# Cached attention on one core: two quarters of wo between the last V blocks, and row sums in two wide products

## The chip, the cores and the metric

The kernel runs on one core of a Trainium2 chip. The metric is the time of one execution in device microseconds, the median over several runs; less is better. The profile is one execution recorded by the hardware profiler; its times are counted from the first instruction, and the span from the first to the last instruction is a little shorter than the time of the execution.

## The reference

Grouped attention over a cache, for 8 sequences of 4 new tokens each. 32 query heads share 8 K/V heads of width 128, with 2048 cached positions. All is bfloat16.

```python
B, Sq, D = 8, 4, 512
Hq, Hkv, Sk, Dh = 32, 8, 2048, 128

def reference(x, k_cache, v_cache, wq, wo):
    q = (x @ wq).reshape(B, Sq, Hq, Dh).transpose(0, 2, 1, 3)
    k = jnp.repeat(k_cache, Hq // Hkv, axis=1)
    v = jnp.repeat(v_cache, Hq // Hkv, axis=1)
    scores = jnp.einsum("bhqd,bhkd->bhqk", q, k) * (Dh ** -0.5)
    p = jax.nn.softmax(scores, axis=-1)
    o = jnp.einsum("bhqk,bhkd->bhqd", p, v)
    return o.transpose(0, 2, 1, 3).reshape(B, Sq, Hq * Dh) @ wo
```

K and V are 32 MB each, wq and wo 4 MB each; every byte of them is read once. The output is 32 KB.

## The kernel before

**Units and steps.** Two K/V heads of one sequence make a unit: 32 units, numbered u, ordered by head pair p (4 of them, `G2`) and then by sequence b (8). A unit's K is one tile of 128 partitions by 32 columns of 128 values (`k_sb`, 1 MB, one DMA, line 87), and its V the same (`v_sb`, line 97). A unit is worked in two halves of 16 columns. The main loop (line 264) runs over `step`, one half of a unit in each: 64 steps (`NH`) and a lead of 7. In one step TensorE transposes K of half `step + 7` (`transpose_part`, line 163, in two parts), computes the scores of half `step + 6` (line 179), and, with the exponentials ready by then, the values of half `step` (line 199). In the second half of a unit it first computes the row sums (`norms`, line 213), and after the values VectorE normalises (`finish`, line 230).

**The engines.** The order on each engine is the order of the text; the schedule is manual. The transposed K goes from PSUM to SBUF as `kt` by VectorE (line 168), and in one of four cases by ScalarE (line 166). ScalarE computes the exponentials into `probs` (line 185). The scores are written with the positions on the partitions, so the sum over positions is a product of `probs` with a matrix of ones: it gives every partition the same sums. `norms` takes the 32 columns of a unit in groups of `LC = 8`, each group one product of 256 columns accumulated into `l_ps`; VectorE then adds the 8 groups (line 221) and takes the reciprocal (line 225).

**The output projection.** When a head pair is done, `to_tokens` (line 242) transposes its eight heads to have tokens on the partitions and copies them to `nat_sb` (line 248), and `to_wo_rows` (line 257) transposes them back with the rows in the order in which wo is loaded, copied to `oP[p]` (line 262). For the first three pairs this is done in the main loop, in the steps of the next pair's second and third sequence. `project` (line 297) multiplies `oP[p]` with quarter p of wo, eight products of 512 columns, all accumulated into `out_ps`.

**The loads.** All go through SyncE's queue, in the order of a list: K of unit u together with V of unit u - 3, from one list that runs until all V are in. `load_ready` is called at the end of each step and lets out what has a free buffer: 7 for K, 6 for V. At most eight DMAs are under way. When the list is empty (step 51), the loads of wo follow: three of 1 MB, one of 512 KB and two of 256 KB (`load_wo`, line 104). After the loop stand the last pair's transposes, the 32 products of `project`, two casts (lines 313 and 314) and the store.

PSUM is used in four pools: `psum_k` for the transposed K (3 buffers), `psum_s` for scores and for `out_ps` (2), `psum_o` (2), and `psum_l` (1) for the row sums, `nat` and `perm` in turn.

Of the kernel before, what the change touches and what calls it, by code (L numbers as in the profile page):

```python
# [9 lines left out]
FP32 = mybir.dt.float32  # L10
# [4 lines left out]
def kernel(  # L15
# [9 lines left out]
    nc = tc.nc  # L25

    B, Sq, D = x.shape
    _, Hkv, Sk, Dh = k_cache.shape
# [3 lines left out]
    T = B * Sq  # L32
    R = D // 128
    G2 = Hkv // 2
    C = 2 * Sk // 128
    NQ = 2 * rep * Sq
# [3 lines left out]
    NU = G2 * B  # L40
    NH = 2 * NU
# [4 lines left out]
    WR = HP  # L46
    DH = D // 2
    AX = mybir.AxisListType.X
    LC = 8
    ADD = mybir.AluOpType.add  # L50
    assert Dh == 128 and C == 32 and NQ == 32

    const = ctx.enter_context(tc.tile_pool(name="const", bufs=1))
    kpool = ctx.enter_context(tc.tile_pool(name="kpool", bufs=KB))
# [4 lines left out]
    psum_s = ctx.enter_context(tc.tile_pool(name="psum_s", bufs=2, space=bass.MemoryType.PSUM))  # L59
# [11 lines left out]
    wo_sb = const.tile([128, G2, WR, D], BF16, name="wo_sb")  # L71
    out_sb = const.tile([T, D], BF16, name="out_sb")
    oP = [const.tile([128, WR, T], BF16, name=f"oP{p}") for p in range(G2)]
# [28 lines left out]
    def load_wo(p, r0, n):  # L102
        rows = wo[p * HP * 128 : (p + 1) * HP * 128, :].rearrange("(q r) j -> q r j", r=WR)
        nc.sync.dma_start(wo_sb[:, p, r0 : r0 + n, :], rows[:, r0 : r0 + n, :])
# [3 lines left out]
    loads = []  # L108
    for u in range(NU + KA):
        if u < NU:  # L110
            loads.append(("k", u))
        if u >= KA - 1 and u - KA + 1 < NU:
            loads.append(("v", u - KA + 1))
    loads.reverse()

    def load_ready(nk, nv):

        while loads:
            kind, u = loads[-1]
            if u >= (nk + KB if kind == "k" else nv + VB):  # L120
                return
            loads.pop()
            (load_k if kind == "k" else load_v)(u)

    load_ready(0, 0)

    make_identity(nc, ident[:])
# [10 lines left out]
    for p in range(G2):  # L138
        psq = psum_s.tile([128, HP, T], FP32, tag="s", name="psq")
        for h in range(HP):  # L140
            hh = p * HP + h
            for r in range(R):
                nc.tensor.matmul(  # L143
                    psq[:, h, :],
                    lhsT=wq_sb[:, r, hh * 128 : (hh + 1) * 128],
                    rhs=xT_sb[:, r, :],
                    start=(r == 0),
                    stop=(r == R - 1),
# [9 lines left out]
    def transpose_part(i, part):  # L158
        u, hf = divmod(i, 2)
        c0 = hf * HC + part * (HC // 2)  # L160
        kp = psum_k.tile([128, HC // 2, 128], BF16, tag="k", name="kp")
        for c in range(HC // 2):
            nc.tensor.transpose(kp[:, c, :], ks[u][:, c0 + c, :], ident[:, :])  # L163
        k_t = ktpool.tile([128, HC // 2, 128], BF16, tag="kt", name="kt")
        if part == 1 and hf == 1:
            nc.scalar.copy(out=k_t[:, :, :], in_=kp[:, :, :])  # L166
        else:
            nc.vector.tensor_copy(out=k_t[:, :, :], in_=kp[:, :, :])  # L168
        kt[(i, part)] = k_t

    def scores(i):
        u, hf = divmod(i, 2)
        p, b = units[u]
        pr = probs[u % len(probs)]
        s_ps = psum_s.tile([128, HC, NQ], FP32, tag="s", name="s_ps")
        q2 = qT_all[:, p, b, :, :].rearrange("d h s -> d (h s)")
        for c in range(HC):
            k_t = kt[(i, c // (HC // 2))]
            nc.tensor.matmul(  # L179
                s_ps[:, c, :], lhsT=k_t[:, c % (HC // 2), :], rhs=q2, start=True, stop=True  # L180
            )
        for g in range(2):
            rows = slice(g * 64, (g + 1) * 64)
            cols = slice(g * NQ // 2, (g + 1) * NQ // 2)
            nc.scalar.activation(  # L185
                out=pr[rows, hf * HC : (hf + 1) * HC, cols], in_=s_ps[rows, :, cols], func=EXP
            )
# [3 lines left out]
    def values(i):  # L191
        u, hf = divmod(i, 2)
        p, b = units[u]
        pr = probs[u % len(probs)]
        if hf == 0:
            o_ps[u] = psum_o.tile([128, NQ], FP32, tag="o", name="o_ps")
        for c in range(HC):
            cc = hf * HC + c
            nc.tensor.matmul(  # L199
                o_ps[u][:, :],  # L200
                lhsT=vs[u][:, cc, :],
                rhs=pr[:, cc, :],
                start=(cc == 0),
                stop=(cc == C - 1),
            )
# [3 lines left out]
    def norms(u):  # L209
        pr = probs[u % len(probs)]  # L210
        l_ps = psum_l.tile([128, LC, NQ], FP32, tag="l", name="l_ps")
        for c in range(0, C, LC):
            nc.tensor.matmul(  # L213
                l_ps[:, :, :],
                lhsT=ones[:, :],
                rhs=pr[:, c : c + LC, :],
                start=(c == 0),
                stop=(c + LC == C),
            )
        l_sb = small.tile([128, NQ], FP32, tag="l_sb", name="l_sb")  # L220
        nc.vector.tensor_reduce(  # L221
            out=l_sb[:, :], in_=l_ps[:, :, :].rearrange("d c q -> d q c"), axis=AX, op=ADD
        )
        r_sb = small.tile([128, NQ], FP32, tag="r_sb", name="r_sb")
        nc.vector.reciprocal(r_sb[:, :], l_sb[:, :])  # L225
        r_sbs[u] = r_sb

    def finish(u):
        p, b = units[u]
        nc.vector.tensor_tensor(  # L230
            out=oT_all[:, p * HP : (p + 1) * HP, b, :],
            in0=o_ps[u][:, :].rearrange("d (h s) -> d h s", h=HP),
            in1=r_sbs[u][:, :].rearrange("d (h s) -> d h s", h=HP),
            op=mybir.AluOpType.mult,
        )
# [3 lines left out]
    def to_tokens(p):  # L239
        nat = psum_l.tile([T, HP, 128], BF16, tag="l", name="nat")  # L240
        for h in range(HP):
            nc.tensor.transpose(  # L242
                nat[:, h, :],
                oT_all[:, p * HP + h, :, :].rearrange("d b s -> d (b s)"),
                ident[:, :],
            )
        nat_sb = small.tile([T, HP * 128 // WR, WR], BF16, tag="nat_sb", name="nat_sb")
        nc.vector.tensor_copy(  # L248
            out=nat_sb[:, :, :].rearrange("t q r -> t (q r)"),
            in_=nat[:, :, :].rearrange("t h d -> t (h d)"),  # L250
        )
        nats[p] = nat_sb

    def to_wo_rows(p):
        perm = psum_l.tile([128, WR, T], BF16, tag="l", name="perm")
        for r in range(WR):
            nc.tensor.transpose(
                perm[:, r, :],
                nats[p][:, :, :].rearrange("t q r -> t r q")[:, r, :],
                ident[:T, :T],  # L260
            )
        nc.vector.tensor_copy(out=oP[p][:, :, :], in_=perm[:, :, :])

    for step in range(-L - 1, NH):
        i, j = step + L + 1, step + L
        if i < NH:
            transpose_part(i, 0)
        if 0 <= j < NH:
            scores(j)
        if i < NH:  # L270
            transpose_part(i, 1)
        u, hf = divmod(step, 2)
        if step >= 0:
            p, b = units[u]
            if hf == 1:
                norms(u)
            values(step)
            if hf == 1:
                finish(u)
            elif p > 0 and b == 1:  # L280
                to_tokens(p - 1)
            elif p > 0 and b == 2:
                to_wo_rows(p - 1)
        load_ready(min((i + 1) // 2, NU), max((step + 1) // 2, 0))
        if step == NH - 1 - 2 * VB:
            assert not loads
            for w in range(G2 - 1):
                load_wo(w, 0, WR)
            load_wo(G2 - 1, 0, 4)
            load_wo(G2 - 1, 4, 2)  # L290
            load_wo(G2 - 1, 6, 2)

    out_ps = psum_s.tile([T, D], FP32, tag="s", name="out_ps")

    def project(p, r0, n):
        for r in range(r0, r0 + n):
            nc.tensor.matmul(  # L297
                out_ps[:, :],
                lhsT=oP[p][:, r, :],
                rhs=wo_sb[:, p, r, :],  # L300
                start=(p == 0 and r == 0),
                stop=(p == G2 - 1 and r == WR - 1),
            )

    to_tokens(G2 - 1)
    project(0, 0, WR)
    to_wo_rows(G2 - 1)
    for p in range(1, G2 - 1):
        project(p, 0, WR)
    project(G2 - 1, 0, 4)  # L310
    project(G2 - 1, 4, 2)
    project(G2 - 1, 6, 2)
    nc.vector.tensor_copy(out=out_sb[:, :DH], in_=out_ps[:, :DH])  # L313
    nc.scalar.copy(out=out_sb[:, DH:], in_=out_ps[:, DH:])  # L314
    nc.sync.dma_start(out=out.flatten_outer_dims(), in_=out_sb[:, :])
# [30 lines left out]
```

The softmax here doesn't subtract the row's maximum and nothing guards it: scores larger than these inputs give would overflow.

## Time and profile before

| | |
|---|---|
| Runs | 194.17, 194.27, 196.10, 196.83 us; median 195.18 |
| The profiled execution | 194.17 us, span 192.2 us, mean granted clock of TensorE 0.991 |
| Busy | TensorE 147.9 us (77%), weight loads 136.4 (71%), VectorE 99.3 (52%), ScalarE 83.9 (44%), GpSimd 0.7 |
| DMA | 76.03 MB, mean 396 GB/s over the span; 413 to 428 in the stationary part |
| The chain that ended last | DMA 94%, TensorE 3% |
| K blocks, V blocks | 32 and 32 of 1 MB, 20.2 us from issue to landing |
| wo | 1 MB three times (20.9 us to landing), 512 KB (19.7), 256 KB twice (16.3) |

How to read the lines that follow. A timeline line has the start, the duration, the engine, the line of the code, the operation, what is written and read, the shapes and how many; the bracket is idle time of that engine before it, and what ended it. In the chain's lines, the start and the duration are followed by what held the end up. In the groups of instructions, the busy time and the mean of one in nanoseconds stand after the first bar, the idle time before them after the second. PE is TensorE, PEld its weight loads, DVE VectorE, ACT ScalarE, SPq the queue of SyncE, L213 line 213.

### The profile page before, as it was taken

How to read it: one execution, taken by the hardware profiler on the slowest of the kernel's cores; microseconds unless marked ns; L12 is line 12 of the kernel's file. 1: busy time of each engine (PE TensorE's matmuls, PEld its weight loads, DVE VectorE, ACT ScalarE, POOL GpSimd, SP SyncE). 2: the span in 40 equal slices, each digit the busy share in tenths (PEclk: the TensorE clock that was granted, in tenths of full speed). 3: DMA queues.
4: the chain of work that ended last, by engine and by line, in shares of the span. 5: the costliest groups of instructions: out<-in, count | busy, mean ns of one | idle time of the engine just before them, and what ended most of it. 6: DMA issues, size and time to landing. Idle time of an engine off the chain costs nothing.

```text
span 192.2 us, 7489 instructions
## 1 busy us (share of the span) xinstructions
PE 147.9 (77%) x3428; PEld 136.4 (71%) x3428; DVE 99.3 (52%) x211; ACT 83.9 (44%) x166; POOL 0.7 (0%) x6
## 2 busy tenths in 40 slices
PE   1019777899989887987778899869877799786793
PEld 0019776888878786877777888859877788775541
DVE  6001645656756565655555557635655576555300
ACT  2003567556555553555554444445555544460000
POOL 1000000000000000000000000000000000000000
PEclk9999999999999999999999999988999999999999
DMA  6989999999999999999999999999999999999930
GB/s 225 436 378 424 421 423 418 423 413 421 418 418 413 423 413 424 416 421 414 421 421 418 416 419 421 418 418 414 421 418 421 414 428 414 419 413 424 376 159 7
DMA packets 10351, 76.03 MB, mean 396 GB/s; under 512 B 1168, under 2 KB 1232, under 8 KB 1616
## 3 DMA queue, kind: packets, MB, share of 16 engines
q1 hardware_dynamic: 10320, 75.57, 94.9%
q8 instruction: 26, 0.43, 0.9%
q14 instruction: 5, 0.04, 0.1%
HBM read 75.53 MB, written 0.03 MB: 393 GB/s over the span
## 4 chain that ended last, share of the span: by engine, by line
DMA 94%; PE 3%; SPq 1%; issue 0%; DVE 0%; ACT 0%
DMA k_sb<-in_k_cache_dram 73%; DMA wo_sb<-in_wo_dram 11%; DMA v_sb<-in_v_cache_dram 10%; PE out_ps L297 2%; PE kp L163 1%; PE l_ps L213 0%; DVE out_sb L313 0%; SPq L87 0%; SPq L107 0%; PE s_ps L179 0%; PE o_ps L199 0%; SPq L106 0%; ACT out_sb L314 0%
## 5 line engine op out<-in xcount | busy, mean ns | idle before, releaser
L168 DVE COPY kt<-kp 128x1024 bf16<-128x1024 bf16 x96 | 65.8, 688 | 66.9 <-PE kp L163 66.1
L163 PE MATMUL kp<-ident,k_sb 128*128 128x128 bf16 x1024 | 78.8, 221 | 17.7 <-DMA k_sb<-in_k_cache_dram 17.2
L185 ACT ACTIVATE probs<-s_ps 64x256 bf16<-64x256 f32 x128 | 48.3, 378 | 74.0 <-PE s_ps L179 73.3
L163 PEld LDWEIGHTS <-k_sb 128*128 128x128 bf16 x1024 | 59.5, 98 | 20.9 <-DMA k_sb<-in_k_cache_dram 19.8
L179 PE MATMUL s_ps<-qT_all,kt 128*128 128x32 bf16 x1024 | 38.2, 177 | 6.7 <-ACT kt L166 5.5
L179 PEld LDWEIGHTS <-kt 128*128 128x128 bf16 x1024 | 33.3, 96 | 8.2 <-ACT kt L166 6.8
L199 PE MATMUL o_ps<-probs,v_sb 128*128 128x32 bf16 x1024 | 35.9, 177 | 2.4 <-DMA v_sb<-in_v_cache_dram 2.0
L199 PEld LDWEIGHTS <-v_sb 128*128 128x128 bf16 x1024 | 33.6, 96 | 3.1 <-DMA v_sb<-in_v_cache_dram 2.2
L166 ACT COPY kt<-kp 128x1024 bf16<-128x1024 bf16 x32 | 32.4, 1012 | 0.8
L213 PE MATMUL l_ps<-probs,ones 128*128 128x256 bf16 x128 | 19.6, 277 | 0.0
L221 DVE TENSOR_REDUCE l_sb<-l_ps 128x32 f32<-128x256 f32 x32 | 13.3, 416 | 5.0 <-PE l_ps L213 4.9
L213 PEld LDWEIGHTS <-ones 128*128 128x128 bf16 x128 | 11.2, 99 | 1.1 <-issue 0.3
L225 DVE RECIPROCAL r_sb<-l_sb 128x32 f32<-128x32 f32 x32 | 11.3, 353 | 1.1
L143 PE MATMUL psq<-xT_sb,wq_sb 128*128 128x32 bf16 x128 | 3.6, 188 | 9.6 <-DMA wq_sb<-in_wq_dram 9.6
L143 PEld LDWEIGHTS <-wq_sb 128*128 128x128 bf16 x128 | 3.5, 104 | 9.7 <-DMA wq_sb<-in_wq_dram 9.7
L230 DVE TENSOR_TENSOR oT_all<-o_ps,r_sb 128x32 bf16<-128x32 f32 x32 | 6.1, 192 | 3.3
L297 PE MATMUL out_ps<-wo_sb,oP 128*32 128x512 bf16 x32 | 7.4, 379 | 0.4 <-DMA wo_sb<-in_wo_dram 0.4
L150 ACT ACTIVATE qT_all<-psq 128x256 bf16<-128x256 f32 x4 | 1.5, 383 | 14.1 <-PE psq L143 14.1
L314 ACT CAST out_sb<-out_ps 32x256 bf16<-32x256 f32 x1 | 0.4, 361 | 16.3 <-DVE out_sb L313 16.3
L297 PEld LDWEIGHTS <-oP 128*32 128x32 bf16 x32 | 3.0, 97 | 3.9 <-issue 0.7
L248 DVE COPY nat_sb<-nat 32x1024 bf16<-32x1024 bf16 x4 | 2.7, 679 | 3.1 <-PE nat L242 3.1
L313 DVE CAST out_sb<-out_ps 32x256 bf16<-32x256 f32 x1 | 0.4, 412 | 5.6 <-PE out_ps L297 5.6
(17 smaller groups left out, 16.4 us busy)
## 6 DMA issues: line engine op xcount, KB each, us to landing
k_sb<-in_k_cache_dram SPq DMA_DIRECT2D x32, 1024.0 KB, 20.2
v_sb<-in_v_cache_dram SPq DMA_DIRECT2D x32, 1024.0 KB, 20.2
wq_sb<-in_wq_dram SPq DMA_DIRECT2D x1, 4096.0 KB, 12.4
wo_sb<-in_wo_dram SPq DMA_DIRECT2D x3, 1024.0 KB, 20.9
wo_sb<-in_wo_dram SPq DMA_DIRECT2D x1, 512.0 KB, 19.7
wo_sb<-in_wo_dram SPq DMA_DIRECT2D x2, 256.0 KB, 16.3
x_sb<-in_x_dram SPq DMA_DIRECT2D x1, 32.0 KB, 1.8
out_dram<-out_sb SPq DMA_DIRECT2D x1, 32.0 KB, 1.5
```

The source lines that it names most:

```text
L143: nc.tensor.matmul(psq[:, h, :], lhsT=wq_sb[:, r, hh * 128 : (hh + 1) * 128], rhs=xT_sb[:, r, :], start=(r == 0), stop=(r == R - 1),)
L163: nc.tensor.transpose(kp[:, c, :], ks[u][:, c0 + c, :], ident[:, :])
L166: nc.scalar.copy(out=k_t[:, :, :], in_=kp[:, :, :])
L168: nc.vector.tensor_copy(out=k_t[:, :, :], in_=kp[:, :, :])
L179: nc.tensor.matmul(s_ps[:, c, :], lhsT=k_t[:, c % (HC // 2), :], rhs=q2, start=True, stop=True)
L185: nc.scalar.activation(out=pr[rows, hf * HC : (hf + 1) * HC, cols], in_=s_ps[rows, :, cols], func=EXP)
L199: nc.tensor.matmul(o_ps[u][:, :], lhsT=vs[u][:, cc, :], rhs=pr[:, cc, :], start=(cc == 0), stop=(cc == C - 1),)
L213: nc.tensor.matmul(l_ps[:, :, :], lhsT=ones[:, :], rhs=pr[:, c : c + LC, :], start=(c == 0), stop=(c + LC == C),)
L221: nc.vector.tensor_reduce(out=l_sb[:, :], in_=l_ps[:, :, :].rearrange("d c q -> d q c"), axis=AX, op=ADD)
L225: nc.vector.reciprocal(r_sb[:, :], l_sb[:, :])
L230: nc.vector.tensor_tensor(out=oT_all[:, p * HP : (p + 1) * HP, b, :], in0=o_ps[u][:, :].rearrange("d (h s) -> d h s", h=HP), in1=r_sbs[u][ ...
L297: nc.tensor.matmul(out_ps[:, :], lhsT=oP[p][:, r, :], rhs=wo_sb[:, p, r, :], start=(p == 0 and r == 0), stop=(p == G2 - 1 and r == WR - 1),)
```

## The change

Two quarters of wo are put into the list of loads between the last three V blocks: V of unit 29, quarter 0, V of unit 30, quarter 1, V of unit 31. `load_ready` lets a quarter of wo out without asking for a buffer. Quarters 2 and 3 follow after the list, in the same pieces as before. `project(0)` is done in the loop at step 59, after the values of unit 29, and `project(1)` at step 61, after those of unit 30; `out_ps` is taken there. After the loop, half of `project(2)` stands between the two transposes of the last pair, and the other half behind them. The row sums are taken in groups of 16 columns instead of 8, so two products of 512 columns instead of four of 256, and the reduction behind them reads 16 groups.

```diff
--- before.py
+++ after.py
@@ -46,9 +46,9 @@
     WR = HP
     DH = D // 2
     AX = mybir.AxisListType.X
-    LC = 8
+    LC = 16
     ADD = mybir.AluOpType.add
-    assert Dh == 128 and C == 32 and NQ == 32
+    assert Dh == 128 and C == 32 and NQ == 32 and G2 == 4
 
     const = ctx.enter_context(tc.tile_pool(name="const", bufs=1))
     kpool = ctx.enter_context(tc.tile_pool(name="kpool", bufs=KB))
@@ -111,12 +111,18 @@
             loads.append(("k", u))
         if u >= KA - 1 and u - KA + 1 < NU:
             loads.append(("v", u - KA + 1))
+        if u in (NU, NU + 1):
+            loads.append(("wo", u - NU))
     loads.reverse()
 
     def load_ready(nk, nv):
 
         while loads:
             kind, u = loads[-1]
+            if kind == "wo":
+                loads.pop()
+                load_wo(u, 0, WR)
+                continue
             if u >= (nk + KB if kind == "k" else nv + VB):
                 return
             loads.pop()
@@ -260,6 +266,16 @@
                 ident[:T, :T],
             )
         nc.vector.tensor_copy(out=oP[p][:, :, :], in_=perm[:, :, :])
+
+    def project(p, r0, n):
+        for r in range(r0, r0 + n):
+            nc.tensor.matmul(
+                out_ps[:, :],
+                lhsT=oP[p][:, r, :],
+                rhs=wo_sb[:, p, r, :],
+                start=(p == 0 and r == 0),
+                stop=(p == G2 - 1 and r == WR - 1),
+            )
 
     for step in range(-L - 1, NH):
         i, j = step + L + 1, step + L
@@ -284,32 +300,23 @@
         load_ready(min((i + 1) // 2, NU), max((step + 1) // 2, 0))
         if step == NH - 1 - 2 * VB:
             assert not loads
-            for w in range(G2 - 1):
-                load_wo(w, 0, WR)
-            load_wo(G2 - 1, 0, 4)
-            load_wo(G2 - 1, 4, 2)
-            load_wo(G2 - 1, 6, 2)
-
-    out_ps = psum_s.tile([T, D], FP32, tag="s", name="out_ps")
-
-    def project(p, r0, n):
-        for r in range(r0, r0 + n):
-            nc.tensor.matmul(
-                out_ps[:, :],
-                lhsT=oP[p][:, r, :],
-                rhs=wo_sb[:, p, r, :],
-                start=(p == 0 and r == 0),
-                stop=(p == G2 - 1 and r == WR - 1),
-            )
-
-    to_tokens(G2 - 1)
-    project(0, 0, WR)
-    to_wo_rows(G2 - 1)
-    for p in range(1, G2 - 1):
-        project(p, 0, WR)
-    project(G2 - 1, 0, 4)
-    project(G2 - 1, 4, 2)
-    project(G2 - 1, 6, 2)
+            load_wo(2, 0, WR)
+            load_wo(3, 0, 4)
+            load_wo(3, 4, 2)
+            load_wo(3, 6, 2)
+        if step == NH - 5:
+            out_ps = psum_s.tile([T, D], FP32, tag="s", name="out_ps")
+            project(0, 0, WR)
+        elif step == NH - 3:
+            project(1, 0, WR)
+
+    to_tokens(3)
+    project(2, 0, 4)
+    to_wo_rows(3)
+    project(2, 4, 4)
+    project(3, 0, 4)
+    project(3, 4, 2)
+    project(3, 6, 2)
     nc.vector.tensor_copy(out=out_sb[:, :DH], in_=out_ps[:, :DH])
     nc.scalar.copy(out=out_sb[:, DH:], in_=out_ps[:, DH:])
     nc.sync.dma_start(out=out.flatten_outer_dims(), in_=out_sb[:, :])
```

## The prediction

> **What bounds the kernel now.** I read the page's busy slices and DMA queues first, then the chain of waits from 160 us, then the timeline from 174 us. All times "at" are microseconds from the span's start. A block is 1 MB: one K or V tile, or a quarter of wo.
>
> ```profile
> DMA  6989999999999999999999999999999999999930
> q1 hardware_dynamic: 10320, 75.57, 94.9%
> ...
> 144.41 20.07 DMA v_sb<-in_v_cache_dram
> 164.49 20.87 DMA wo_sb<-in_wo_dram
> 185.40 3.63 PE out_ps L297 x16
> 189.05 0.42 DVE out_sb L313
> ```
>
> The DMA engines are full from the second slice to the last but two, and one queue holds 94.9% of their time. The chain is transfers until 185.36, when the third quarter of wo lands. Only then does TensorE set the end: 16 products in 3.63 us, then two casts (0.42 and 0.36 us) and the store. So the change can win or lose in two places: in the time the stream takes, and in what is left to do at its end.
>
> ```profile
> 175.51 0.56 PE L199 MATMUL o_ps<-probs,v_sb 128*128 128x32 bf16 x16 [0.92 <-DMA v_sb<-in_v_cache_dram]
> ...
> 178.00 0.57 PE L199 MATMUL o_ps<-probs,v_sb 128*128 128x32 bf16 x16 [1.09 <-DMA v_sb<-in_v_cache_dram]
> 178.41 0.60 PE L213 MATMUL l_ps<-probs,ones 128*128 128x256 bf16 x4
> 178.85 0.55 PE L199 MATMUL o_ps<-probs,v_sb 128*128 128x32 bf16 x16
> 179.05 0.42 DVE L221 TENSOR_REDUCE l_sb<-l_ps 128x32 f32<-128x256 f32 x1 [1.39 <-PE l_ps L213]
> 179.51 0.35 DVE L225 RECIPROCAL r_sb<-l_sb 128x32 f32<-128x32 f32 x1
> 179.97 0.19 DVE L230 TENSOR_TENSOR oT_all<-o_ps,r_sb 128x32 bf16<-128x32 f32 x1
> ...
> 180.67 1.89 PE L297 MATMUL out_ps<-wo_sb,oP 128*32 128x512 bf16 x8
> 180.87 0.68 DVE L248 COPY nat_sb<-nat 32x1024 bf16<-32x1024 bf16 x1 [0.71 <-PE nat L242]
> 182.49 0.67 PE L257 MATMUL perm<-ident,nat_sb 32*128 32x32 bf16 x8
> 183.20 0.29 DVE L262 COPY oP<-perm 128x256 bf16<-128x256 bf16 x1 [1.65 <-PE perm L257]
> 185.40 3.61 PE L297 MATMUL out_ps<-wo_sb,oP 128*32 128x512 bf16 x16 [0.41 <-DMA wo_sb<-in_wo_dram]
> ```
>
> Two V blocks start 2.50 us apart (175.50, 178.00, both ended by a landing). The third quarter of wo lands 7.36 us after the last V block: three blocks, 2.45 us each. The last quarter then lands at about 187.8 (estimate from the same step). After the last V block TensorE needs until 183.49 to have oP3, and that whole row of work lies under three landings. Between a product and the next there are (3.61 - 0.38) / 15 = 0.216 us.
>
> **The change, part by part.**
>
> *Stream.* The same 75.57 MB in the same number of DMAs. The queue lets one go about every 2.5 us, with 20.2 us from issue to landing, so moving two issues (0.33 us each on SP) ahead of two V blocks moves only which block lands when. In the waits of SP's queue, V loads wait 3.0 us in all for o_ps, up to 2.3 at once; in the timeline that longest one is the last V block's, issued at 159.40 instead of about 157.0. A quarter of wo needs no freed buffer and will be issued in that gap. I cost this at nothing, either way: the late block landed 2.50 us after the one before it, so the queue had not run dry. POOL's queue carries none of this. New landings, from the old places in the row: first quarter of wo 175.50, next-to-last V 178.00, second quarter 180.45, last V 182.90, third quarter 185.36, last quarter about 187.8. The last V block comes 4.90 us later; the stream's end does not move.
>
> *The two early projections.* Eight products at 0.216 are 1.73 us of TensorE. The first group starts when its quarter lands (175.50; TensorE is through with the V block before at 174.6) and ends at 177.23, 0.77 us ahead of the next V block. The second runs 180.45 to 182.18, 0.72 us ahead of the last V block. So they cost nothing; the transfers hide them. What is queued behind their waits on TensorE is the next V block's products, which wait for a transfer behind the quarter on the same queue. If a cover of 0.7 us were gone, the rest of TensorE's row would slip one for one.
>
> *Row sums.* Four products of 256 columns become two of 512, and two weight loads per unit go. Old: 4 in 0.60 us, so 0.108 apart. New, by the row of the projection (512 columns, 0.216 apart, 0.38 long): 0.60 us again, so nothing on TensorE. The reduce reads 512 values instead of 256.
>
> ```profile
> L213 PE MATMUL l_ps<-probs,ones 128*128 128x256 bf16 x128 | 19.6, 277 | 0.0
> L221 DVE TENSOR_REDUCE l_sb<-l_ps 128x32 f32<-128x256 f32 x32 | 13.3, 416 | 5.0 <-PE l_ps L213 4.9
> ```
>
> No row shows a reduce of 512. The bounds are 0.416 (length costs nothing) and 0.832 (all of it scales). A copy of 128x32 on VectorE takes 0.151 us, so I take 0.15 as fixed and the remaining 0.27 as scaling: 0.68, or +0.27 a unit (0 to +0.42). Over 32 units that is 8.5 us of VectorE, hidden in all but the last: a unit lasts about 4.97 us, VectorE is busy 2.9 to 3.5 of it, TensorE 4.0 to 4.6, and TensorE waits 17.2 us in all for K blocks. What is late next is the kt copy behind the normalisation (145.09, needed by scores at 147.33): 0.68 long, so 1.5 us of cover.
>
> *The tail.* Everything from the last V block on is now a chain under two landings instead of four. Steps of before, shifted by 4.90: products of V at 182.90, reduce at 183.95, +0.27, normalisation at 185.14, transposes to tokens at 185.38 (before: 180.21). After 0.46 TensorE is free (185.84); half of the third quarter's products, 4 x 0.216 = 0.86, takes it to 186.70 (the quarter is there since 185.36). The copy nat_sb runs 186.04 to 186.72, so these products are hidden by it. The second transposes start 0.09 later than TensorE is free, as before, at 186.80; 0.60 later the other four products (0.86) start, ending their slots at 188.26, by when oP3 (186.80 + 0.71 + 0.29 = 187.80) is ready and the last quarter has landed. Then eight products, 7 x 0.216 + 0.38 = 1.89: **190.15 against 189.03**, +1.1 us. From there on nothing differs. Of the 1.1, 0.27 is the reduce; without the wide sums it would be about +0.85. The bounds of the reduce make it +0.85 to +1.3. The landings shown step by 2.45 to 2.50, which moves it by 0.1.
>
> *Sum.* The profiled execution took 194.17 us (span 192.2): 195.3. The four runs go from 194.17 to 196.83 with the median at 195.18, so this execution is the fastest of them; put on the median it is **196.3**, 0.6% longer.
>
> **A row that speaks against the change.** [...] Split into 3.41 us stretches, the granted clock is 1.00 from 18.9 us on in all but one:
>
> ```profile
> 73.50:76.92 3.42, 2.09 (x53) 1.89 (x50) 1.19 (x2) 1.46 (x3) 0.00 (x0) 1.00 1.01 419
> 124.70:128.11 3.41, 1.69 (x49) 1.59 (x47) 0.55 (x2) 1.60 (x4) 0.00 (x0) 1.00 1.03 420
> 128.11:131.52 3.41, 3.41 (x56) 3.15 (x54) 2.49 (x6) 1.02 (x4) 0.00 (x0) 0.50 1.00 418
> ```
>
> Columns: stretch, length, busy time of TensorE, weight loads, VectorE, ScalarE, GpSimd, then clock and DMA. After a stretch with TensorE busy for 1.69 us the clock is half for the next 3.41 us; after 2.09 us it stays full. The longest idle time in the stretch that lost the clock was 1.72 us. The new tail has such thin stretches: 179.40 to 182.81 holds only the second projection (1.89 us), and 182.37 to 185.78 holds the last V block's products and sums (1.40) and 0.40 of transposes, 1.80. [...]
>
> **The rivals.**
>
> *The clock halves in the tail (slower).* Place: one of the two thin stretches. Price: in the half-clock stretch the four sums took 0.85 us of TensorE instead of 0.44 (128.28 to 129.13), 16 value products 0.47 instead of 0.40, eight transposes 0.81 instead of 0.45. After the first thin stretch that is 0.07 + 0.41 + 0.36 plus 0.27 for the last sum's own length: +1.1, so +2.2, 197.4. After the second it meets the transposes and most of the last 12 products, about 3 us more: +4.1, 199.3. Middle: about 198.3. It decides if the limit lies above some 1.8 to 1.9 us of busy time (the rows leave 1.69 to 2.09 open) and a stretch falls so. Against it: stretches start where they will, and most positions show over 2.1 us. The kernel before has such a stretch too (176.91 to 180.32, 1.5 us), but there the wait for wo hides a slow TensorE.
>
> *VectorE becomes the bound (slower).* If the longer reduce lay on the loop's path, 31 x 0.27 = 8.4 us would come on top: about 204.7. For it: the reduce, reciprocal, normalisation and kt copy run back to back at 144.08 to 145.77. Against it: 1.5 us of cover, and the K waits of TensorE.
>
> *The tail stays hidden (not slower).* If the chain after the last V block were 1.7 us shorter than I count, the end would be the last landing and the last two products, 187.8 + 0.22 + 0.38 = 188.4: 0.6 us less than before, 194.6. Against it: every step above is a row of the trace. This is also the most that the reordering could win while the stream is as long as it is; faster by over 1% would need a shorter stream, and nothing removes bytes.
>
> **How the numbers follow.** Forecast 0.68 (of it 0.08 above 1%, from the reduce's bound and the spread of runs), clock 0.17, VectorE 0.03, hidden tail 0.12 (of it 0.04 a shorter stream). One per cent, 1.95 us, is about what a measurement can tell from no change. Faster 0.04, within 1% 0.68, slower 0.28. Time 196.3. Range 194.6 (hidden tail; or this forecast on the quickest of the runs shown, less a cheap reduce) to 198.6 (the middle of the clock case, or the forecast on the longest of the runs shown).
>
> **What would show it.** Right: last V block's products start near 182.9, reduces last 0.68, sums 0.60 for two, first projections end about 0.7 us before the V blocks land, TensorE unbroken from about 185.4 to 190.15, the chain passing from v_sb to TensorE and VectorE instead of wo_sb. Wrong: a wait for wo_sb in the last eight products, K waits of TensorE gone (VectorE bound), a clock of 0.50 after 182 us, or a last landing away from 187.8.

## The result and the profile after

The changed kernel takes 196.26 us (median of 43 runs, 195.15 to 197.08), the kernel before 195.66 (64 runs, 194.13 to 197.07). The ratio is 1.0031, with a 95% interval from 1.0015 to 1.0048: a little slower, by less than the 0.6% of the forecast. The shortest runs are 1.0 us apart, the longest are alike.

The profiled execution took 196.59 us, one of the longer ones. Its chain of waits from the last V block's load on (start, duration, what held the end up):

```profile
162.02 20.93 DMA v_sb<-in_v_cache_dram
...
183.00 0.57 PE o_ps L205 x16
183.56 0.45 PE l_ps L219 x2
...
184.04 0.70 DVE l_sb L227
...
184.77 0.36 DVE r_sb L231
...
185.22 0.20 DVE oT_all L236
...
185.47 1.03 PE nat L248 x8
186.51 1.71 PE out_ps L272 x4
188.21 0.61 PE perm L263 x8
188.82 2.75 PE out_ps L272 x12
```

The last transfer in the chain is now the last V block, which lands at 182.95, and not a quarter of wo. Behind it stands a row of TensorE and VectorE work, 8.6 us long, ending at 191.57. Up to 185.47 each step starts within 0.1 us of the time worked out. Then two steps are too long: the transposes to tokens (1.03 us; 0.62 before) and the next four products (1.71; 0.86 at 0.216 each). The stretches of 3.41 us, cut where the clock changes and in equal steps back from there, show why (columns as in the prediction: TensorE's busy time first after the length, the granted clock third from the end):

```profile
175.22:178.63 3.41, 1.84 (x23) 0.90 (x22) 0.35 (x2) 0.00 (x0) 0.00 (x0) 1.00 1.00 417
178.63:182.05 3.42, 2.28 (x25) 1.30 (x24) 1.24 (x3) 0.00 (x0) 0.00 (x0) 1.00 0.96 388
182.05:185.46 3.41, 1.77 (x36) 1.06 (x34) 1.24 (x3) 0.00 (x0) 0.00 (x0) 1.00 0.53 210
185.46:188.87 3.41, 3.40 (x21) 1.97 (x22) 0.69 (x2) 0.00 (x0) 0.00 (x0) 0.50 0.15 58
```

The stretch from 182.05 was thin (1.77 us), and the next had half the clock. So this execution shows the forecast and its first rival together.

The queue of the stream moves 75.57 MB in 10320 packets, as before. The groups of instructions have the reduce of 512 values at 682 ns:

```profile
L227 DVE TENSOR_REDUCE l_sb<-l_ps 128x32 f32<-128x512 f32 x32 | 21.8, 682 | 8.8 <-PE l_ps L219 3.6 <-remote 3.4 <-PE s_ps L185 1.7
```

The timeline of the two places where TensorE waits for the stream:

```profile
180.53 1.89 PE L272 MATMUL out_ps<-wo_sb,oP 128*32 128x512 bf16 x8 [1.08 <-DMA wo_sb<-in_wo_dram]
183.00 0.57 PE L205 MATMUL o_ps<-probs,v_sb 128*128 128x32 bf16 x16 [0.58 <-DMA v_sb<-in_v_cache_dram]
```

The second early projection waits 1.08 us for its quarter, and TensorE is idle again for 0.58 us before the last V block, so the projection was hidden.

Two questions were left. Is the spread of the runs, in both kernels, the clock? And what do the two halves of the change, the order and the wide sums, cost by themselves? Theory A says that the end is set by the chain worked out, and that the clock stretches it in some executions. Rival B lays the spread on late transfers; the others are named where they are met.

### The profile page after: what moved, and what is told of

The parts are those of the page before. It is cut to its first block, busy times and chain, and to the rows that moved or that the text cites. A ratio compares the mean times of both kernels' runs of the same rounds, so it can differ in the third digit from the quotient of the medians.

```text
span 194.8 us, 7331 instructions
## 1 busy us (share of the span) xinstructions
PE 147.2 (76%) x3334; PEld 130.4 (67%) x3364; DVE 107.6 (55%) x211; ACT 83.9 (43%) x166; POOL 0.7 (0%) x6
## 3 DMA queue, kind: packets, MB, share of 16 engines
q1 hardware_dynamic: 10320, 75.57, 93.7%
## 4 chain that ended last, share of the span: by engine, by line
DMA 93%; PE 4%; DVE 1%; SPq 1%; issue 0%; ACT 0%; DVEq 0%
DMA k_sb<-in_k_cache_dram 82%; DMA v_sb<-in_v_cache_dram 11%; PE out_ps L272 2%; PE nat L248 1%; DVE l_sb L227 0%; PE perm L263 0%; PE o_ps L205 0%; PE l_ps L219 0%; SPq L87 0%; DVE out_sb L320 0%; SPq L107 0%; SPq L106 0%; DVE r_sb L231 0%; ACT out_sb L321 0%; DVE oT_all L236 0%
## 5 line engine op out<-in xcount | busy, mean ns | idle before, releaser
L169 PE MATMUL kp<-ident,k_sb 128*128 128x128 bf16 x1024 | 78.3, 221 | 17.1 <-DMA k_sb<-in_k_cache_dram 16.6
L227 DVE TENSOR_REDUCE l_sb<-l_ps 128x32 f32<-128x512 f32 x32 | 21.8, 682 | 8.8 <-PE l_ps L219 3.6
L219 PE MATMUL l_ps<-probs,ones 128*128 128x512 bf16 x34 | 12.8, 386 | 1.3 <-issue 0.2
L272 PE MATMUL out_ps<-wo_sb,oP 128*32 128x512 bf16 x32 | 8.5, 412 | 1.1 <-DMA wo_sb<-in_wo_dram 1.1
L219 PEld LDWEIGHTS <-ones 128*128 128x128 bf16 x64 | 5.0, 99 | 0.1
L248 PE MATMUL nat<-ident,oT_all 128*32 128x128 bf16 x32 | 2.9, 243 | 1.1 <-DVE oT_all L236 1.1
```

Of the source, the lines that this page charges most:

```text
L219: nc.tensor.matmul(l_ps[:, :, :], lhsT=ones[:, :], rhs=pr[:, c : c + LC, :], start=(c == 0), stop=(c + LC == C),)
L227: nc.vector.tensor_reduce(out=l_sb[:, :], in_=l_ps[:, :, :].rearrange("d c q -> d q c"), axis=AX, op=ADD)
L272: nc.tensor.matmul(out_ps[:, :], lhsT=oP[p][:, r, :], rhs=wo_sb[:, p, r, :], start=(p == 0 and r == 0), stop=(p == G2 - 1 and r == WR - 1),)
```

## The experiments

**The clock held, changed kernel.** Products of 512 columns, written into a PSUM buffer of the pool of the transposed K and read by nobody, fill TensorE's waits in the tail. Kernels with such products are called warmed below.

```diff
+    def warm(n):
+        w_ps = psum_k.tile([128, 512], FP32, tag="k", name="w_ps")
+        for _ in range(n):
+            nc.tensor.matmul(
+                w_ps[:, :], lhsT=ones[:, :], rhs=wq_sb[:, 0, :512], start=True, stop=True
+            )
...
             project(0, 0, WR)
+            warm(3)
         elif step == NH - 3:
+            warm(3)
             project(1, 0, WR)
+            warm(2)
+    warm(4)
     to_tokens(3)
```

> The changed kernel with 12 products of 512 columns whose result nobody reads, put where TensorE waits in the tail (3 behind the first projection, 3 before and 2 behind the second, 4 before the last transposes). Theory A (the end is the chain behind the last V block, and the spread of the runs comes from the clock halving in that chain): every run keeps clock 1.00 from 176 us on, the chain from the first product of the last V block to the last projection is 7.2 to 7.3 us instead of the 8.6 of the profile after, the runs lie near 195.2 us, the median goes from 196.3 to 195.2. Rival B (the spread comes from the stream of transfers, which lands late in some runs): the added products change nothing, the median stays at 196.3 with runs from 195.1 to 197.1.

Median 195.34 us, 12 runs from 195.15 to 195.77; ratio to before 0.9982 (0.9954 to 1.0010). The chain of waits and the stretches of the tail:

```profile
182.99 0.56 PE o_ps L205 x16
...
185.46 0.62 PE nat L248 x8
186.08 0.86 PE out_ps L272 x4
186.94 0.60 PE perm L263 x8
187.54 2.71 PE out_ps L272 x12
```

```profile
179.40:182.80 3.40, 2.96 (x14) 0.97 (x11) 0.90 (x3) 0.00 (x0) 0.00 (x0) 1.00 0.86 346
182.80:186.20 3.40, 3.08 (x48) 1.93 (x49) 1.32 (x4) 0.00 (x0) 0.00 (x0) 1.00 0.49 194
186.20:189.60 3.40, 3.40 (x22) 1.68 (x21) 0.89 (x2) 0.00 (x0) 0.00 (x0) 1.00 0.05 19
```

At full clock the last product ends at 190.25, 7.26 us after the first product of the last V block. The prediction had 182.90 to 190.15, 7.25. More work on TensorE made the kernel quicker, and its upper runs are gone (195.77 at most, where 27 of the 43 runs of the changed kernel took more). Rival B falls. That the clock was full throughout the tail is seen in the profiled execution alone; of the other runs only the mean over the span is recorded, 0.98 to 1.00.

**The clock held, kernel before.**

```diff
...
+        if step == NH - 5:
+            warm(2)
+        elif step == NH - 3:
+            warm(3)
...
+    warm(3)
     to_tokens(G2 - 1)
```

> The kernel before with 8 such products in the waits of its tail (2, 3 and 3). Theory A: the upper runs go, the median falls from 195.7 to about 194.2, the ratio is 0.992 to 0.994, and the two warmed kernels then differ by the 1.1 us of the chain that was worked out. Rival B: median 195.7 and runs from 194.1 to 197.1 as before.

Median 194.37 us, 11 runs from 194.25 to 194.55; ratio to before 0.9929 (0.9903 to 0.9955), where the kernel before had 196.02 on the same chip (34 runs, 194.20 to 196.92). The end of its chain is that of the profile before, only with wo 0.2 us later:

```profile
164.30 21.26 DMA wo_sb<-in_wo_dram
...
185.60 3.63 PE out_ps L308 x16
```

The upper runs are gone here too. Of those 34 runs, the 18 whose mean granted clock was 0.974 or less all took 195.93 us or more; the 12 shortest, up to 195.79, all had 0.982 or more. The remaining four had 0.982 or more and still took 195.98 to 196.92; in one of them (196.48) the span was 193.5 us, so about 1 us of its time lay outside the span. So the clock accounts for most of the spread, not for every run, and no long execution of the kernel before was profiled. In the changed kernel the mean clock does not part the runs (0.990 and 0.991 go with 195.15 to 196.56 us), and of the two half stretches in its profile one, at 127.43, is far from the tail. There the profile and the added products carry the claim. The two warmed kernels do not overlap: 195.34 / 194.37 = 1.0050, 0.97 us.

**The wide sums alone.**

```diff
-    LC = 8
+    LC = 16
```

> The kernel before with the row sums in two wide products, and nothing else. Theory A: the reduce takes 0.68 instead of 0.42 us, the normalisation of the last unit comes 0.27 later, and this is hidden, since oP3 is then ready near 183.8 and the products wait for wo until 185.4: ratio 1.000, within 0.002. Rival C (VectorE's 8.5 us lie on the loop's path): up to 8 us more. Rival D (the 0.27 comes through to the end): ratio 1.0014.

Median 196.07, ratio 1.0007 (0.9979 to 1.0034); rival C falls. But no run was under 195.13, and a few should have been near 194.2. Its profile happens to show what a halved clock does to the old order. Stretches, then the end of the chain:

```profile
175.26:178.67 3.41, 1.26 (x34) 1.01 (x34) 1.49 (x5) 0.00 (x0) 0.00 (x0) 1.00 1.00 416
178.67:182.08 3.41, 2.37 (x28) 1.67 (x27) 1.44 (x4) 0.00 (x0) 0.00 (x0) 0.50 0.96 386
182.08:185.50 3.42, 3.42 (x13) 1.20 (x12) 0.48 (x1) 0.00 (x0) 0.00 (x0) 0.50 0.52 208
```

```profile
180.81 1.03 PE nat L242 x8
181.84 3.41 PE out_ps L297 x8
185.26 0.60 PE perm L257 x8
185.86 5.30 PE out_ps L297 x24
```

With half the clock for 6.8 us, the first eight products take 3.41 us instead of 1.73, and 24 products are left at 185.86, where at full clock 16 are left at about 185.4 to 185.8. TensorE ends at 191.16; the loads of wo are no longer in the chain at all.

**The wide sums alone, clock held.** `LC = 16` in the warmed kernel before.

> The kernel before, with the wide row sums and the same 8 added products in the waits of the tail. Theory A: with the clock held the longer reduce is hidden under the landings of wo, so the runs lie with those of the warmed kernel before, 194.4 us within 0.1. Rival D (the 0.27 of the reduce comes through, which is why no run of the wide sums alone was under 195.1): 194.6 or more, without a halved clock.

Median 194.30 (194.05 to 194.48), against 194.37 without them, on another chip. The chain does not pass through the reduce, but through the third quarter of wo:

```profile
164.58 21.25 DMA wo_sb<-in_wo_dram
...
185.87 3.63 PE out_ps L308 x16
```

The copy behind the second transposes ends at 183.60, 2.2 us before that landing (185.83). So the reduce is hidden, as worked out, and rival D falls. Whether the wide sums make thin stretches more frequent without the added products is open; 12 runs don't settle it.

**The order alone, without and with the clock held.** `LC = 8` in the changed kernel, and in the warmed changed kernel.

> The changed kernel with the row sums in four products of 256 columns as before; only the order of the loads and projections is changed. Theory A: the chain behind the last V block is 0.27 shorter than in the changed kernel, 7.0 us at full clock; the shortest runs are near 194.9 (before 194.1, changed 195.15), the median, moved by the clock too, near 196.0. Rival E (the reduce has nothing to do with the end, the order alone makes the 1.1): shortest runs 195.15.

> The changed order of loads and projections with row sums of 256 columns and the same 12 added products. Theory A: the chain behind the last V block is 7.05 us, 0.27 less than with the wide sums; median about 195.05, so that the 1.0 us between the two warmed kernels parts into some 0.7 from the order and 0.27 from the reduce, which counts only in the new order. Rival E: 195.3, as with the wide sums.

Unwarmed: median 195.70 (194.91 to 196.75), ratio 0.9994 (0.9962 to 1.0026). Its chain, at full clock in this execution, is short by the reduce:

```profile
183.32 0.57 PE o_ps L205 x16
...
184.37 0.44 DVE l_sb L227
...
187.63 2.71 PE out_ps L272 x12
```

From 183.32 to 190.33 it is 7.01 us, 0.25 less than with the wide sums. Warmed, the median is 195.27 (195.09 to 195.57), only 0.07 under the 195.34 with wide sums, so here the expectation of 195.05 was missed. The chain was 7.0 us in that profile too (183.49 to 190.49), but the last V block came 0.5 us later than in the other (182.99). Whether that lateness is chance or comes with the narrow sums is not shown. By the times, rival E's 195.3 is what came: on one chip the new order with narrow sums is 0.97 us longer than the old order with hidden wide sums (195.27 and 194.30), and on the other chip the new order with wide sums is 0.97 longer than the old one with narrow sums (195.34 and 194.37). So the times show that the order alone costs about 0.97 us with the clock held. The 0.27 of the reduce shows in the chain (7.26 against 7.01 and 7.00), not in the times.

**Loads early, projections late.** The two quarters of wo stay between the V blocks; all 32 products go behind the loop.

```diff
-        if step == NH - 5:
-            out_ps = psum_s.tile([T, D], FP32, tag="s", name="out_ps")
-            project(0, 0, WR)
-        elif step == NH - 3:
-            project(1, 0, WR)
...
+    out_ps = psum_s.tile([T, D], FP32, tag="s", name="out_ps")
     to_tokens(3)
-    project(2, 0, 4)
+    project(0, 0, WR)
     to_wo_rows(3)
-    project(2, 4, 4)
+    project(1, 0, WR)
+    project(2, 0, WR)
```

> The changed kernel with the two quarters of wo still loaded between the V blocks, but all 32 products of the projection behind the loop, in the order of the kernel before. Theory A: the chain behind the last V block (182.9) then holds 32 products instead of 16: tokens at 185.4, eight products in the place of the copy's time, transposes at 187.7, and 24 products behind them, the end of the last at about 193.5 instead of 190.2 at full clock: 3.3 us more than the changed kernel, about 199 to 200 us. Rival F (the early projections matter little, the place of the loads is all): 196.3.

Four runs from 200.97 to 201.31, median 201.05; ratio 1.0281 (1.0234 to 1.0327). More than the 199 to 200 expected, and the profile says by what: TensorE has nothing to do between the V blocks, and the clock is half for 10.2 us.

```profile
179.34:182.75 3.41, 0.28 (x11) 0.17 (x7) 1.14 (x3) 0.00 (x0) 0.00 (x0) 0.50 0.87 354
182.75:186.17 3.42, 1.98 (x36) 1.33 (x37) 1.24 (x3) 0.00 (x0) 0.00 (x0) 0.50 0.51 201
186.17:189.59 3.42, 3.42 (x15) 1.74 (x16) 0.68 (x1) 0.00 (x0) 0.00 (x0) 0.50 0.04 15
```

TensorE ended at 196.02 instead of 193.5. Of these 2.5 us, 0.25 is the start on the last V block (183.15 for 182.90). Most of the rest stands in steps under the halved clock: sums 0.87 for 0.45 us, transposes 1.03 for 0.62, the first eight products 3.01 for 1.73, together 2.1. So the early projections are worth 3.3 us by the sum, and about 2.1 more against a kernel that holds the clock; rival F falls.

**A smaller change to the old order.** In the warmed kernel before, the third quarter of wo comes in two pieces, so that its first four products need not wait for the whole:

```diff
-            for w in range(G2 - 1):
+            for w in range(G2 - 2):
                 load_wo(w, 0, WR)
+            load_wo(G2 - 2, 0, 4)
+            load_wo(G2 - 2, 4, 4)
```

> The kernel before (all of wo behind V, sums of 256 columns) with the 8 added products, and the third quarter of wo loaded in two pieces of 512 KB instead of one. Theory A: the last 16 products no longer wait for the whole quarter at 185.4 but begin at about 184.9 with its first half, and the end is set by the last landing (187.9 to 188.1) and two products: 0.4 to 0.6 us less than the warmed kernel before, 193.8 us, ratio to before 0.990. Rival G (a further DMA costs the stream as much as it gives): 194.4.

Median 193.87 (193.62 to 194.61), ratio to before 0.9925 (0.9893 to 0.9956), and 0.50 under the warmed kernel before (194.37), which was timed on another chip. On the same chip the warmed kernel before with wide sums, whose reduce is hidden, had 194.30, so 0.43 is the safer figure. Rival G's 194.4 did not come. In its chain all the last 24 products are one row of TensorE, with a short wait inside, and end at 188.90 (189.22 in the warmed kernel before):

```profile
182.88 0.60 PE perm L257 x8
183.48 5.42 PE out_ps L310 x24
```

This is the quickest of all the versions run, ahead of both kernels.

> The kernel before with the third quarter of wo in two pieces, without the added products. Theory A: the shortest runs are 0.5 us under those of the kernel before (193.6), but the clock takes as much from the longer ones as before, since a slow TensorE, not the landing, then sets the end: median 195.2 to 195.7, ratio 0.997 to 1.000, with the whole 0.5 seen only where the clock is held (193.87 with the added products). Rival H (the split helps whatever the clock does): median 0.5 under that of the kernel before.

Without the added products: median 195.93 (193.95 to 196.22), ratio 1.0013 (0.9987 to 1.0039). The median gains nothing, so rival H falls. The expectation was missed too: the shortest run is 0.12 under the shortest of the kernel before on this chip (194.07), not 0.5, and the median lies above 195.7. It agrees with the view that the earlier landing gains only where TensorE is not late; why the shortest runs gained so little is open.

**The kernel before once more.**

> The kernel before, unchanged, profiled once more, to see one of its longer executions. Theory A: if this execution takes 195.5 us or more, the clock is 0.50 for at least one stretch of 3.4 us between 178 and 187 us, the last V block still lands at 178.0 within 0.3, and the last 16 products start behind 185.4 because TensorE is late and not because wo is. If it takes 194.2 to 194.5, there is no halved clock behind 178 us. Rival B: a longer execution shows the third quarter of wo landing later than 185.9.

This execution took 194.54 us, a short one. Its mean clock is 0.991, that of the profile before, where one stretch was halved, and from 178 us on its products take the times of the full clock (four sums 0.60 us, transposes 0.62, eight products 1.89); its last 16 products start at 185.79, 0.04 after the third quarter's landing. It agrees with theory A and does not test it, since a long one was wanted. It was 0.37 us longer than the profile before, and the quarter landed 0.39 later (185.75 for 185.36): some tenths of the spread do come from the landings, as rival B has it, but no more than that is seen.

## Why the prediction was right, and where it was off

*The number.* 196.3 against a measured 196.26 is closer than the working deserves, and that is luck. The sum set +1.1 on a median of four runs, 195.18; over 64 runs the kernel before has 195.66, and the median moved by 0.60. A base 0.48 too low and a step 0.5 too large cancelled. What was right is the chain.

*The stream.* Right. The last V block landed at 182.95 (182.90 worked out). In none of the profiles with the new order did the last eight products wait for wo.

*The two early projections.* Right that they cost nothing. The covers differed: the first began at 174.58, since its quarter was there sooner, and left 1.57 us; the second left 0.58 (0.72 worked out).

*Row sums.* Right: two products in 0.59 us, the reduce 0.682 (0.68). VectorE's busy time rose by 8.3 us (99.3 to 107.6), TensorE's wait for K blocks is 16.6 us (17.2 before), so the loop did not feel it.

*The tail.* Right: 7.26 us at full clock against 7.25 of the sum. With the clock held the whole change costs 0.97 us, where the sum had 1.1; by the times the order alone has all of it, where the sum had 0.85 for the order and 0.27 for the reduce.

*The clock.* Here a step failed. The prediction gave it 0.17 as a rival and wrote that in the kernel before "the wait for wo hides a slow TensorE". It does not: in the old order with wide sums, with half the clock from 178.67, 24 products were left when 16 should be, and the mean clocks and the warmed kernel say that most runs of the kernel before lose 1 to 2 us to the clock. The halved clock is thus the usual case of both kernels and not a rival to one. So the median moved by 0.6 us and not by the 0.97 of the warmed kernels: the old order loses more to the clock (196.02 to 194.37 on one chip, 1.65 us) than the new one (196.26 to 195.34, 0.9, these two not timed together). That the early projections pay back a part of what the order costs, by filling waits of the old tail, fits this; the kernel with late projections, with half the clock for 10.2 us, speaks for it.

The new tail did not lose its clock in every execution: in the profile after, the stretch from 182.05 held 1.77 us of work (1.80 worked out) and was followed by half the clock, while in the profile of the order alone TensorE was busy for about 2.0 of the 3.41 us before the transposes at 185.54, and these took 0.62 us, as at full clock. That the place of the stretches decides it is the author's estimate. The second term that was mis-sized is the price in the new tail after the late thin stretch, about 3 us. In the profile after, it was 0.41 for the transposes and 0.85 for four products, 1.3 in all, because the stretch of half clock was over when the last twelve products began. One such stretch could not have cost 3 us: the most that half the speed takes from 3.41 us is 1.7.

The hidden tail did not happen: the chain was as long as its rows say. VectorE did not become the bound.

## What to carry to other kernels

Where transfers set the pace, count what a load ahead of the last input block does to that block's landing. Here two quarters of wo put ahead of it moved its first products from 178.00 to 183.00 us, two steps of 2.50, and what depends on it became a chain under two landings instead of four: add up that chain, step by step, against the transfers still behind it. And before a tail is reordered, look at the granted clock there. In this kernel TensorE had half the clock (0.50 from 185.46 to 188.87 in the profile after) just when it had become the bound, after waits that nothing filled: products that nobody reads, put into those waits, were worth 1.65 us by the medians (1.4 by the ratio), more than the 0.97 us that the new order cost.

## What the runs showed of the hardware that was not expected

- The granted clock changed at steps of 3.41 us: in the profile after at 127.43, 130.84, 185.46 and 188.87, which lie 1, 17 and 18 such steps behind the first. In other executions the changes lay elsewhere (the first halving in the loop came at 128.11 in the profile before, at 132.70 in that of the warmed kernel before with wide sums). Among the stretches at full clock, those in which TensorE was busy for 1.26 us (wide sums alone), 1.69 (before), 1.77 (after) and 1.83 (the warmed kernel before with wide sums) were followed by half the clock, and those with 1.84 and 1.86 (after) and 2.09 (before) kept it. But in a second profiled execution of the kernel before (194.98 us) one with 2.07, from 176.40, was followed by half the clock, and one with 2.05, from 74.00, kept it. So a busy time that parts the two was not shown; no stretch was made to probe for one, and not every product is recorded (of the wide sums of the changed kernel 34 of 64). The stretch with 1.83 and the next, and the one with 1.86; the one with 1.84, from 175.22, is shown above:

```profile
129.29:132.70 3.41, 1.83 (x52) 1.73 (x50) 1.36 (x4) 1.77 (x3) 0.00 (x0) 1.00 1.01 418
132.70:136.11 3.41, 3.19 (x54) 2.85 (x53) 2.43 (x4) 0.76 (x2) 0.00 (x0) 0.50 1.02 418
```

```profile
59.17:62.58 3.41, 1.86 (x34) 1.60 (x36) 0.93 (x3) 1.58 (x3) 0.00 (x0) 1.00 1.00 413
```

- The longest single wait did not decide it: in the profile after the stretch from 182.05 had none over 1.08 us and lost the clock, the one from 175.22 had one of 1.57 us and kept it. Stretches at half the clock with 1.98 and 2.37 us busy were followed by half the clock again (late projections, wide sums alone), one with 3.19 us, from 127.43 in the profile after, by the full one.
- The halved clock did not slow all work alike: products of 512 columns doubled (four in 1.71 us instead of 0.86), the second transposes did not change (0.61 us under half the clock in the profile after, 0.60 at the full one), and 16 products of 32 columns took 0.61 us instead of 0.56 (the kernel with the late projections against the warmed one).
- Eight products of no use made the kernel before quicker by 0.7% (ratio 0.9929).
